# A Strassen level more in the second layer: product 4 by small products, its sums made by ScalarE copies and adding DMAs

## The chip, the cores and the metric

The kernel runs on one core of one Trainium2 chip. The metric is the device time of one execution in microseconds. The engines are named as in the profile: PE is TensorE's matmul, PEld its weight load, DVE is VectorE, ACT is ScalarE, POOL is GpSimd, SP is SyncE, which issues most DMAs.

## The reference

A short causal convolution over time with softmax weights, and then a feed-forward layer with the hardswish function. With B = 8, S = 4096, D = 192, 2048 hidden features:

```python
# _attn_ref
w = softmax(weight)                      # 8 heads x 7 taps
out = np.einsum('hk,bskhg->bshg', w, x_unf)   # causal, 7 taps, 24 channels a head
# _moe_ref, x = out as 32768 x 192
h = x @ w_in                             # 192 x 2048
relu6 = np.clip(h + 3.0, 0.0, 6.0)
g = h * relu6 / 6.0
return (g @ w_out).astype(np.float32)    # 2048 x 192
```

All data are float32. The output is 32768 x 192.

## The kernel before, in words

The tokens are cut into 32 blocks of 1024 (`TB`), each in two halves of 512 (`N`). Block 0 runs on its own path, overlapped with the rounding of the weights. Each of the other 31 blocks has two stretches on TensorE: the first layer (`first_layer`, matmuls of line 432) and the second layer (`second_layer`, line 528).

First layer: the convolved tokens `y` are split into a high and a low part in `y_own` (`split_high` on ScalarE, `split_rest` on VectorE, lines 859 to 863), copied to the other half of the partitions in `y_other` by DMA (`swap_parts`), and multiplied by the parts of `w_in` in 16 units. Units 0 to 7 read `y_own`, units 8 to 15 `y_other`. A unit takes one of four PSUM slots (two banks each); ScalarE takes the relu (line 306), VectorE the gate (line 310), and the result lies in `g`. `g` has four quarters by half of the hidden features and half of the tokens: A11, A21, A12, A22, each 8 chunks of 128 features by 512 tokens. Units 0 to 7 fill A11 and A22, units 8 to 15 A21 and A12.

Second layer: `g @ w_out` by one level of Strassen's method (Winograd's form) over the four quarters of `g` and of `w_out`: seven products of 512 tokens by 96 outputs by 1024 features. The sums of quarters are S1 (in A21's place), S2 (in A11's), S3 and later S4 (in a tile of their own, `S3`). GpSimd makes S3 for the first three pairs of chunks (`g_sums`, lines 468 and 380), VectorE for the last; S1 = A21 + A22 is made by two adding DMAs issued by GpSimd (line 470) and two additions on VectorE (line 472). The sums of weights are made once.

TensorE's array is used as four groups of 32 columns, each with its own 32 rows of PSUM: streams 0 to 3 (`tile_position=(0, j * QS)`). Streams 0, 1 and 2 compute rows 0-31, 32-63 and 64-95 of the products 4, 7, 2, 6 and 3, a matmul of 512 tokens (`plain`) counting as two steps. Products 1 and 5 are cut once more by the same method, in stream 3 (`level_two`): their rows 0-63 as seven small products of 256 tokens and 4 matmuls (`small`, four steps each), rows 64-95 plain. The small products 1 and 2, for one, add onto the same PSUM rows (A), with a copy of A to another place (B) between them. Pieces move between rows of PSUM by ScalarE copies (`copy`, lines 525 and 608 to 611) and VectorE additions (line 400).

The order is written out by hand. `put` gives each matmul the step at which its stream has come to it (`clock`), `do(t, ...)` places a copy, sum or store at step t, less a half. All are sorted by step, stably, and issued in that order; each engine then runs its own in order. The framework adds the semaphore waits from what each instruction reads and writes. Every stream has 82 steps. The second layer uses three of the four PSUM slots, six banks named d, e, b, x_, a and c; B, C and V are rows 96-127 of x_, d and b, A and E rows 96-127 of e and a. In product 1, rows 64-95 are begun by stream 3 in V, copied into e and continued by streams 0, 1 and 2 in turn, each time with a copy of e's rows to the next stream's rows.

Between the matmuls `second_layer` also issues the next block's `split_high`, `split_rest` and `swap_parts` (steps 13, 15 and 18), the small sums of S1 into A22's place for product 5 (`small_sums`, line 637, on VectorE), S2 and S4 (lines 641 and 642, step 38), and what finishes each output.

Of the kernel before, what the change touches and what calls it, by code (L numbers as in the profile page):

```python
# [31 lines left out]
def kernel(  # L32
# [8 lines left out]
    nc = tc.nc  # L41
# [27 lines left out]
    ys = ctx.enter_context(tc.tile_pool(name="ys", bufs=1))  # L69
    ot = ctx.enter_context(tc.tile_pool(name="ot", bufs=1))  # L70
# [50 lines left out]
    y_own = [cst.tile([P, K3, N], F32, name=f"y{n}") for n in range(2)]  # L121
# [4 lines left out]
    w_s = cst.tile([P, 2, 4, NP // 2, QS], F32, name="w_s")  # L126

# [314 lines left out]

    def first_layer(i, jobs):
# [11 lines left out]
        count = 2 * NP  # L455
        for job in jobs.get(-1, ()):
            job()
        for n in range(count):
            unit(n)
            for job in jobs.get(n, ()):  # L460
                job()
# [4 lines left out]
            if n > NP and n % 2:  # L466
                pair = slice(n - NP - 1, n - NP + 1)
                g_sums(nc.gpsimd if n + 1 < count else nc.vector, (3,), range(NP)[pair], 2)
# [24 lines left out]
    def small_weights(to, w):  # L493

        b11, b12, b21, b22 = (
            w_out[:, c::2, w, q * QS : (q + 1) * QS] for c in range(2) for q in range(2)
        )
        t1, t2, t3, t4 = (to[:, n] for n in range(4))
        for o, p, q in ((t1, b12, b11), (t2, b22, t1), (t3, b22, b12), (t4, b21, t2)):
            nc.gpsimd.tensor_tensor(out=o, in0=p, in1=q, op=ALU.subtract)  # L500

    def second_layer(i, between):
        last = i + 1 == NB
        ours = [free_slots.pop(0) for _ in range(3)]
        d, e, b, x_, a, c = (psum[:, 2 * n + k] for n in ours for k in range(2))
# [36 lines left out]
        def small(n, m_, out, start=False):  # L542

            x, w = prod[n]
            sums, ws = (s1[-1], w_s[:, 0]) if n == 1 else (s5, w_s[:, 1])
            x11, x12, x21, x22 = four_parts(x)
            z1, z2, z3, z4 = four_parts(sums)
# [3 lines left out]
            t1, t2, t3, t4 = (ws[:, k] for k in range(4))  # L551
# [4 lines left out]
            for u in range(NP // 2):  # L556
                put(3, 1, lambda u=u: matmul(
                    3, out[:, lo], wm[:, u], xm[:, u], start and u == 0
# [15 lines left out]

        for q in range(NQ):
            plain(q, d, 4, q, every, True)
            before = (1, 6, NP)[q]
            plain(q, c, 7, q, every[:before], True)
            plain(q, e, 1, 2, range(5 + q, 6 + q))
            do(clock[q], copy, out=e[rows(q + 1)] if q < 2 else p1[third], in_=e[rows(q)])  # L580
            plain(q, c, 7, q, every[before:])
            plain(q, a, 2, q, every[:6], True)
# [8 lines left out]
        def level_two(n, p, chunks, order):  # L591
# [25 lines left out]
            for step in order.split():  # L617
                if step[0] == "x":
                    fill(int(step[1]))
                elif step[0] in "lh":  # L620
# [326 lines left out]
```

## Time and profile before

| what | us |
|---|---|
| median of 3 runs (lowest, highest) | 2220.99 (2220.94, 2223.57) |
| the profiled execution, its time | 2220.6 |
| its span, first to last instruction | 2218.5 |
| matmuls of line 528, busy share of the chain | 50% |
| matmuls of line 432, share of the chain | 47% |
| first layer of one block (983.07 on) | 32.87 |
| second layer of one block (1015.94 on) | 35.47 |
| GpSimd's adding DMA, issue to landing | 5.0 |

The page of the profile gives each engine's busy time, the chain of work that ended last followed back to the start, and groups of like instructions with their mean time and the idle time ahead of them. A timeline row reads: start, length, engine, line of the kernel, operation, tile written <- tile read, shape, count, and in brackets the idle time of that engine just before it and what released it. In a table by stretches the columns are: stretch, its length, then busy time and count for PE, PEld, DVE, ACT and POOL, the granted TensorE clock, the busy share of the DMA engines and GB/s. A queue line gives packets, megabytes and the share of 16 DMA engines' time; an issue line the count, the size and the median time to landing.

### The profile page before, as it was taken

What the parts mean: (1) busy time and instruction counts of PE and PEld (TensorE: products, weight loads), DVE (VectorE), ACT (ScalarE), POOL (GpSimd) and SP (SyncE); (2) the same over time, 40 slices, a digit from 0 to 9 for tenths busy, and PEclk for the clock granted to TensorE, in tenths of its full rate; (3) what the DMA queues carried; (4) which work ended last, traced back from release to release, by engine and by line L of the source; (5) the groups of instructions that cost most, each with busy time, mean ns of one, the idle gap of its engine ahead of it and who ended that gap; (6) DMA issues with size and microseconds to landing.
All of it is one profiled execution on the core that took longest, in us unless ns stands there. A gap on an engine that the chain in (4) does not pass through costs nothing.

```text
span 2218.5 us, 49343 instructions
## 1 busy us (share of the span) xinstructions
PE 2211.4 (100%) x21598; PEld 1535.2 (69%) x21598; DVE 1808.9 (82%) x1588; ACT 935.8 (42%) x1172; POOL 827.9 (37%) x706
## 2 busy tenths in 40 slices
PE   9999999999999999999999999999999999999999
PEld 5567776677776677766777667776667776677766
DVE  8878788888888888888888888888888888888866
ACT  7434443344433444433444334443344433344433
POOL 4434442244422344323444224442244432344322
PEclk9999999999999999999999999999999999999999
DMA  7333323433223332243332333322433224333232
GB/s 165 65 71 69 66 37 67 77 63 77 35 58 78 70 70 49 44 77 70 70 62 40 68 74 66 77 35 59 77 68 73 43 49 77 70 70 57 40 59 34
DMA packets 249095, 142.91 MB, mean 64 GB/s; under 512 B 207120, under 2 KB 212240, under 8 KB 248880
## 3 DMA queue, kind: packets, MB, share of 16 engines
q1 hardware_dynamic: 230392, 105.86, 23.7%
q0 software_dynamic: 17248, 33.64, 8.8%
q8 instruction: 169, 2.77, 0.5%
q10 hardware_dynamic: 1240, 0.27, 0.1%
q14 instruction: 46, 0.38, 0.1%
HBM read 31.72 MB, written 25.17 MB: 26 GB/s over the span
## 4 chain that ended last, share of the span: by engine, by line
PE 99%; ACT 0%; DVE 0%; POOL 0%; DMA 0%; issue 0%; POOLq 0%; ACTq 0%; DVEq 0%
PE psum L528 50%; PE psum L432 47%; PE psum L321 2%; PE psum L730 0%; PE psum L738 0%; ACT g L306 0%; DMA y_other<-y 0%; POOL w_in L220 0%; ACT scale L196 0%; ACT sig L193 0%; ACT sig L199 0%; POOL sig L210 0%; ACT w_in L218 0%; DVE y L283 0%; POOLq L942 0%
## 5 line engine op out<-in xcount | busy, mean ns | idle before, releaser
L528 PE MATMUL psum<-g,w_out 128*32 128x512 f32 (+1 forms) x6712 | 967.4, 552 | 0.0
L306 ACT ACTIVATE g<-psum,half 128x1024 f32<-128x1024 f32 x512 | 572.3, 1118 | 494.0 <-PE psum L432 465.8
L310 DVE SCALAR_TENSOR_TENSOR g<-g,psum 128x1024 f32<-128x1024 f32 x512 | 618.8, 1218 | 195.1 <-ACT g L306 194.8
L491 POOL TENSOR_TENSOR s<-g 128x256 f32<-128x256 f32 x248 | 268.8, 1084 | 1252.5 <-DVE g L310 915.9
L528 PEld LDWEIGHTS psum<-g,w_out 128*32 128x32 f32 x6712 | 370.8, 110 | 246.9 <-issue 126.7
L432 PE MATMUL psum<-y,w_in 64*128 64x512 f32 x4608 | 534.8, 388 | 0.3
L432 PE MATMUL psum<-y_other,w_in 64*128 64x512 f32 x4608 | 529.0, 386 | 0.1
L432 PEld LDWEIGHTS psum<-y,w_in 64*128 64x128 f32 x4608 | 428.6, 184 | 121.3 <-issue 26.0
L432 PEld LDWEIGHTS psum<-y_other,w_in 64*128 64x128 f32 x4608 | 431.6, 184 | 91.1 <-DMA y_other<-y 0.5
L528 PE MATMUL psum<-s,w_out 128*32 128x512 f32 (+1 forms) x3272 | 465.4, 570 | 0.0
L806 DVE SCALAR_TENSOR_TENSOR y<-x,c_sb,y 128x1536 f32<-128x1536 f32 x186 | 334.8, 1800 | 2.1 <-ACT y L804 1.0
L380 POOL TENSOR_TENSOR s<-g 128x1024 f32<-128x1024 f32 x93 | 297.8, 3202 | 25.1 <-DVE g L310 25.1
L528 PE MATMUL psum<-g,w_s 128*32 128x256 f32 x1240 | 282.8, 379 | 0.0
L528 PEld LDWEIGHTS psum<-s,w_out 128*32 128x32 f32 x3272 | 153.7, 110 | 80.1 <-issue 48.3
L528 PEld LDWEIGHTS psum<-g,w_s 128*32 128x32 f32 x1240 | 136.4, 110 | 68.3
L380 DVE TENSOR_TENSOR s<-g 128x2048 f32<-128x2048 f32 (+1 forms) x93 | 177.1, 1931 | 1.1
L528 PE MATMUL psum<-s,w_s 128*32 128x256 f32 x744 | 170.7, 379 | 0.0
L491 DVE TENSOR_TENSOR g<-g 128x1024 f32<-128x1024 f32 x124 | 151.7, 1224 | 5.3
L380 DVE TENSOR_TENSOR g<-g 128x2048 f32<-128x2048 f32 x62 | 139.0, 2283 | 0.0
L400 DVE TENSOR_TENSOR p<-psum,p 32x256 f32<-32x256 f32 (+1 forms) x93 | 47.7, 513 | 96.5 <-PE psum L528 95.1
L400 DVE TENSOR_TENSOR results<-psum,results 32x256 f32<-32x256 f32 (+3 forms) x128 | 69.3, 541 | 50.8 <-issue 47.3
L525 ACT COPY psum<-psum 32x512 f32<-32x512 f32 x93 | 51.3, 551 | 135.4 <-PE psum L528 135.4
(88 smaller groups left out, 1089.1 us busy)
## 6 DMA issues: line engine op xcount, KB each, us to landing
y_other<-y SPq DMA_DIRECT2D x124, 384.0 KB, 4.9
g<-g POOLq DMA_DIRECT2D x62, 512.0 KB, 5.0
out_dram<-results SPq DMA_DIRECT2D x378, 64.0 KB, 2.0
x<-in_x_dram SPq DMA_DIRECT2D x53, 388.5 KB, 7.1
g<-in_moe_w_in_dram SPq DMA_DIRECT2D x16, 192.0 KB, 5.7
stage<-in_moe_w_out_dram SPq DMA_DIRECT2D x8, 384.0 KB, 5.7
x<-in_x_dram SPq DMA_DIRECT2D x7, 384.0 KB, 6.5
y_other<-y SPq DMA_DIRECT2D x12, 128.0 KB, 2.3
```

Source lines behind the costliest of these rows:

```text
L306: nc.scalar.activation(r6, h, ACT.Relu, bias=half[:], scale=1.0 / 6.0)
L310: nc.vector.scalar_tensor_tensor(out=g_, in0=g_, scalar=1.0, in1=h, op0=ALU.min, op1=ALU.mult)
L321: lambda p=p: nc.tensor.matmul(out=bank[j * QS : (j + 1) * QS, tokens], lhsT=w_out[:, p, w, cols], rhs=x[:, p, tokens], start=(first and p ...
L380: engine.tensor_tensor(out=o[:, r], in0=a[:, r], in1=b[:, r], op=op)
L400: nc.vector.tensor_tensor(out=out, in0=x, in1=y, op=op)
L432: nc.tensor.matmul(out=psum[:, 2 * slot + k], lhsT=r32(w_in_parts[wn][r, c, s]), rhs=r32(y_other[r, yn, s] if group else y_own[yn][r, s]), ...
L491: engine.tensor_tensor(out=o, in0=p, in1=q, op=op)
L525: streams[3].append((t - 0.5, lambda: fn(*args, **kw)))
L528: nc.tensor.matmul(out=out, lhsT=w, rhs=x, start=start, stop=True, tile_position=(0, j * QS), skip_group_check=True,)
L806: jobs.append(lambda k=k: nc.vector.scalar_tensor_tensor(out=y[:], in0=x[:, :, k : k + N], scalar=c_sb[:, k : k + 1], in1=y[:], op0=ALU.mu ...
```

## The change

Product 4 (A22 times T4, in streams 0 to 2 plain before, 48 steps) is cut once more too. Its rows 0-63 become seven small products of four steps: 1, 2 and 5 in stream 0, 6 and 3 in stream 1, 7 and 4 in stream 2. Its rows 64-95 stay plain and are made in turn by streams 0, 1 and 2 in bank b (`t4`), with two copies between rows. The pieces are put together in a new SBUF tile `p4`, which is added where bank d was. All streams have 81 steps.

The four small sums of A22 are made while the first layer runs its units 8 to 15: ScalarE copies a quarter with its sign into each sum's buffer (`seed`), GpSimd issues DMAs that add another onto it (`onto`). Two of the four come out with the opposite sign; a third set of small weights, `w_s4`, has the signs turned to match. Two of the buffers lie in the memory of `y_own`, taken after unit 7 and given back after the second layer's use of them, so `split_high`, `split_rest` and `swap_parts` move from steps 13, 15 and 18 to 18, 20 and 23. One S3 pair (unit 11) moves from GpSimd to VectorE. Banks x_ and c change places. The small sums of S1 are made later (steps 22.3, 30.7 and 37), stream 3's first fills go ahead of its small products, the copy of V into e moves from step 14 to 9, and the work from step 32 on comes one step earlier.

```diff
+    w_s4 = cst.tile([P, 5, NP // 2, QS], F32, name="w_s4")
...
+    def sums_a22():
+
+        early = [
+            part[:].rearrange("p s n -> p (s n)")[:, : NP * TH // 2]
+            .rearrange("p (u t) -> p u t", t=TH)
+            for part in z_early or y_own
+        ]
+        return early + [z[:, k] for k in range(2)]
...
+        x11, x12, x21, x22 = four_parts(A22)
+
+        def begin_sums():
+            z_early[:] = own_tiles("z")
+            seed(0, x21, 1.0)
+
+        def seed(k, x, sign):
+            nc.scalar.mul(sums_a22()[k], x, sign)
+
+        def onto(k, x):
+            nc.gpsimd.dma_start(out=sums_a22()[k], in_=x, accum_op=ALU.add)
+
+
+        s4_sums = {
+            NP - 1: [lambda: seed(2, x11, -1.0)],
+            NP: [begin_sums, lambda: onto(2, x21), lambda: onto(0, x22)],
+            NP + 1: [lambda: seed(1, x11, -1.0)],
+            NP + 2: [lambda: seed(3, x12, -1.0), lambda: onto(1, sums_a22()[0])],
+            NP + 6: [lambda: onto(3, sums_a22()[1])],
+        }
...
-                g_sums(nc.gpsimd if n + 1 < count else nc.vector, (3,), range(NP)[pair], 2)
+                g_sums(nc.vector if n in (NP + 3, count - 1) else nc.gpsimd, (3,), range(NP)[pair], 2)
...
-        d, e, b, x_, a, c = (psum[:, 2 * n + k] for n in ours for k in range(2))
+        d, e, b, c, a, x_ = (psum[:, 2 * n + k] for n in ours for k in range(2))
...
+        def plain_half(j, bank, n, q, ch, t, start=False):
             x, w = prod[n]
...
+            put(j, 1, lambda: matmul(
+                j, bank[rows(j), halves[t]], w_out[:, ch, w, q * QS : (q + 1) * QS],
+                x[:, ch, halves[t]], start,
+            ))
...
+            if n == 4:
+                z1, z2, z3, z4 = sums_a22()
+                t1, t2, t3, t4, b22 = (w_s4[:, k] for k in range(5))
...
+        A4, E4, B4, C4 = d[first, lo], d[first, hi], d[second, lo], d[third, lo]
+        t4 = b
...
+        def plain_e(q):
+            plain(q, e, 1, 2, range(5 + q, 6 + q))
+            if q == 2:
+                plain_half(q, e, 1, 2, 4, 1)
+            do(clock[q], copy, out=e[rows(q + 1)] if q < 2 else p1[third], in_=e[rows(q)])
+
+        plain(0, t4, 4, 2, (0,), True)
+        plain_half(0, t4, 4, 2, 1, 0)
+        do(clock[0], copy, out=t4[second], in_=t4[first])
+        small4(0, 1, d[first], True)
+        do(clock[0], copy, out=B4, in_=A4)
+        small4(0, 2, d[first])
+        do(clock[0], copy, out=p4[first, lo], in_=A4)
+        plain_e(0)
+        small4(0, 5, d[first, TH:], True)
+        do(clock[0], copy, out=p4[second, lo], in_=E4)
+        plain(0, c, 7, 0, every, True)
+
+        plain(1, c, 7, 1, every[:3], True)
+        for t, chunks in ((0, (2, 3, 4)), (1, (1, 2, 3, 4))):
+            for ch in chunks:
+                plain_half(1, t4, 4, 2, ch, t)
+        do(clock[1], copy, out=t4[third], in_=t4[second])
+        small4(1, 6, d[second])
+        do(clock[1], copy, out=C4, in_=B4)
+        plain_e(1)
+        plain(1, c, 7, 1, every[3:6])
+        small4(1, 3, d[second])
+        do(clock[1] + 1, add, p4[second, lo], B4, p4[second, lo])
+        plain(1, c, 7, 1, every[6:])
+
+        plain(2, c, 7, 2, every, True)
+        plain(2, t4, 4, 2, (5, 6, 7))
+        do(clock[2], copy, out=p4[third], in_=t4[third])
+        small4(2, 7, d[third])
+        do(clock[2], add, p4[second, hi], C4, p4[second, lo])
+        plain_e(2)
+        plain(2, a, 2, 2, every[:2], True)
+        small4(2, 4, d[third])
+        do(clock[2], copy, out=p4[first, hi], in_=C4)
+        plain(2, a, 2, 2, every[2:6])
+
         for q in range(NQ):
-            plain(q, d, 4, q, every, True)
-            before = (1, 6, NP)[q]
-            plain(q, c, 7, q, every[:before], True)
-            plain(q, e, 1, 2, range(5 + q, 6 + q))
-            do(clock[q], copy, out=e[rows(q + 1)] if q < 2 else p1[third], in_=e[rows(q)])
-            plain(q, c, 7, q, every[before:])
-            plain(q, a, 2, q, every[:6], True)
+            if q < 2:
+                plain(q, a, 2, q, every[:6], True)
+            assert clock[q] == 45
...
-        level_two(1, lambda: p1, range(5), "1 x5 6 5 2 7 3 4")
-        do(14, copy, out=e[first], in_=V)
+        level_two(1, lambda: p1, range(4), "x4 half 1 5 6 2 7 3 4")
+        do(9, copy, out=e[first], in_=V)
...
-        for t, n in ((16.2, 1), (16.2, 2), (30.5, 3), (34.5, 4)):
+        for t, n in ((22.3, 1), (30.7, 2), (30.7, 3)):
...
+        do(37, small_sums, s5, S1, (4,), nc.vector)
...
-        do(62, lambda: add(late["p7"], late["u3"], d[m]))
+        do(61, lambda: add(late["p7"], late["u3"], p4[:]))
...
-                between = [(13, split_high), (15, split_rest), (18, swap_parts)]
+                between = [(18, split_high), (20, split_rest), (23, swap_parts)]
```

## The prediction

> **What bounds the kernel now.** I read the page first: busy shares, then the chain that ended last.
>
> ```profile
> span 2218.5 us, 49343 instructions
> PE 2211.4 (100%) x21598; PEld 1535.2 (69%) x21598; DVE 1808.9 (82%) x1588; ACT 935.8 (42%) x1172; POOL 827.9 (37%) x706
> PE 99%; ACT 0%; DVE 0%; POOL 0%; DMA 0%; issue 0%; POOLq 0%; ACTq 0%; DVEq 0%
> ```
>
> TensorE is the chain; every other engine only has to be in time. The chain listed in order gives the stretches of one block; the table by stretches, cut there, shows what each engine does.
>
> ```profile
> 983.14:1015.94 32.80, 32.80 (x292) 26.83 (x296) 26.97 (x23) 17.32 (x16) 23.59 (x21) 1.00 0.18 30
> 1015.94:1051.40 35.46, 35.46 (x386) 21.11 (x386) 29.19 (x26) 11.08 (x19) 2.04 (x1) 1.00 0.47 94
> ```
>
> First layer 32.8 us, second 35.46 us, clock 1.00. The second layer is written as 82 steps in four streams; 35.46 / 82 = 0.43 us a step, so all four streams are full and nothing stops them. One step less is worth 0.43 us only while that stays so: the question is whether the new order still lets TensorE run without a wait. What a wait costs is read from the tightest place, in the timeline of TensorE, its weight loads and ScalarE.
>
> ```profile
> 1028.34 0.59 PE L528 MATMUL psum<-g,w_out 128*32 128x512 f32 x1
> 1028.77 1.46 PE L528 MATMUL psum<-s,w_out 128*32 128x512 f32 x12
> 1029.01 0.55 ACT L525 COPY psum<-psum 32x512 f32<-32x512 f32 x1 [1.27 <-PE psum L528]
> 1029.61 0.11 PEld L528 LDWEIGHTS psum<-g,w_out 128*32 128x32 f32 x1 [0.23 <-ACT psum L525]
> 1029.62 0.13 PEld L528 LDWEIGHTS psum<-s,w_out 128*32 128x32 f32 x3
> 1029.64 0.59 PE L528 MATMUL psum<-g,w_out 128*32 128x512 f32 x1
> ```
>
> Here the matmul that feeds a copy begins its last pass at 1028.34. The copy starts at 1029.01, ends at 1029.56, and the load that waits for it goes at 1029.61. A matmul right behind the first would have been due at 1028.77 and would have got its weights at 1029.61: a copy with no step between costs 0.85 us. This one has two steps (0.86 us) and costs nothing, by 0.01 us. The row at 1029.62 matters as much: loads of another stream, which need no copy, went only after the waiting one. A wait holds what stands behind it in all four streams.
> The Trainium skill ("TensorE: Matmul & The Clock Gate", Step-by-step) says that TensorE's queue pulls weight loads ahead of matmuls in flight while matmuls keep program order. By that a load behind a waiting one might go early; the row at 1029.62 shows that it didn't.
>
> **The change, part by part.** u is one step, 0.43 us; times are from the start of the second layer. The waits named are those that the changed program has as built: the matmuls' waits on ScalarE's count, instruction by instruction.
>
> *Steps.* Product 4 falls from 48 to 44 steps (7 small products of 4, and 16 plain, for 3 x 16), one step from each stream: -0.43 us.
>
> *More, smaller matmuls.* 17 more a block, 34 more passes. Before, 386 loads of 0.11 us (the load rows of line 528) are 42.5 us in a stretch of 35.46: they overlap each other and the matmuls, and where stream 3 runs small products all the way the step is still 0.43 us. Cost 0.
>
> *Wait at step 4.* The early rows of product 4 are copied from rows 0-31 to rows 32-63 of bank b (the same 0.55 us copy). The copy waits for the count raised after the matmuls of step 2, which end at step 4; stream 3's fill of step 4 writes rows 96-127 of the same bank and, as built, waits for that copy. No step between: 0.85 us.
>
> *Wait at step 7.* Small product 1 of P4 ends there in stream 0; its copy (256 wide, 0.34 us, the row at 1023.88 below) must be done before small product 2 adds onto the same rows, next in the same stream. 0.85 - 0.55 + 0.34 = 0.64 us for stream 0. Streams 2 and 3 next issue at step 8, behind it: 0.64 - 0.43 = 0.21.
>
> *Wait at step 9.* The copy from stream 3's bank-b rows into e, moved from step 14 to 9, is followed at step 9 by stream 1's half matmul into bank b, which waits for it: 0.85 us. Stream 3 is now 0.85 + 0.21 + 0.85 = 1.91 us late, with some 0.1 us of small slips 2.0.
>
> ```profile
> 1018.15 1.48 ACT L415 ACTIVATE y<-y 128x1536 fp32r<-128x1536 f32 x1
> 1023.88 0.34 ACT L610 COPY psum<-psum 32x256 f32<-32x256 f32 x1 [1.10 <-PE psum L528]
> 1025.60 0.37 ACT L611 COPY p<-psum 32x256 f32<-32x256 f32 x1 [0.38 <-PE psum L528]
> 1021.92 1.75 DVE L418 TENSOR_TENSOR y<-y,y 128x1536 fp32r<-128x1536 f32 x1
> 1023.59 2.55 DVE L491 TENSOR_TENSOR g<-g 128x1024 f32<-128x1024 f32 x2
> 1029.15 0.43 DVE L400 TENSOR_TENSOR p<-psum,p 32x256 f32<-32x256 f32 x1 [3.00 <-PE psum L528]
> ```
>
> *split_high, moved from 13 to 18.* Its 1.48 us lay in a gap of ScalarE. Now the buffer is taken by two of the sums until step 17, and behind it on ScalarE stands the copy e[third]<-e[second], which stream 3's small product at step 21 waits for. Three copies due at step 17 wait for matmuls that end at step 18, at 18u + 1.6 (the lag of stream 2) + 0.16 = 9.5; then 0.37 + 0.34 + 0.37 + 1.48 + 0.55 gives 12.6, the matmul 12.7. It is due at 21u + 2.0 = 11.0 to 11.1: 1.6 us.
>
> *What is behind that on VectorE.* split_rest (1.75) follows split_high's end at 12.1; then one small sum (1.22) and the new addition from bank d (0.43): 15.5. Small product 3 of P4, in the same bank at steps 25 to 29, waits for that addition. Stream 3's due time is 26u + 2.0 + 1.6 = 14.8: 0.7 us.
>
> *The sums in the first layer.* Five ScalarE copies of 128x1024 (near the 1.12 us of the relu) in units 7 to 10: relu and copy are 2.2 us against a unit's 2.05, a lag under 1 us, and the next user of a PSUM slot comes four units later. ScalarE waited 465.8 us for TensorE in the relu rows, 15 us a block: 0. The S3 pair moved to VectorE is 1.23 us where VectorE idles 0.8 us a unit (1015.09 in its timeline): 0.
>
> ```profile
> 1010.42 1.20 POOL L470 DMA_DIRECT2D g<-g  x1 [0.30 <-POOL s L380]
> 1011.16 2.89 POOL L380 TENSOR_TENSOR s<-g 128x1024 f32<-128x1024 f32 x1
> q1 hardware_dynamic: 230392, 105.86, 23.7%
> q0 software_dynamic: 17248, 33.64, 8.8%
> g<-g POOLq DMA_DIRECT2D x62, 512.0 KB, 5.0
> ```
>
> *Four adding DMAs on GpSimd.* An issue keeps GpSimd 0.74 us (1010.42 to 1011.16). The third waits for the second's landing, and behind it stands S3's third pair (2.9 us), which stream 2 needs at step 8, 3.4 + 1.0 us late: 4.4. The second is issued at about -9.7 (small sums end at -10.5); landing after 5.0 us, or 10 if it queues behind the first, puts it at -4.7 to 0.3, and the pair's end at 2.1 (as before) to 4.8: 0 to 0.4 us. If their 1 KB pieces took as long each as the 2 KB pieces of before, each transfer would move for 5.4 us in place of 2.7, landing at 3.0 and the pair at 7.5: 3.1 us. The two queue lines speak for size: 0.08 ns a byte with mean pieces of 460 B, 0.09 with 1950 B. I take 0.
>
> *Sum.* 0.85 + 0.21 + 0.85 + 0.1 + 1.6 + 0.7 - 0.43 = +3.9 us for 30 blocks; the last has no split: +1.6. 30 x 3.9 + 1.6 = 118.6. The profiled execution took 2220.6 us, its span 2218.5, as good as the median of 2220.99. Forecast 2220.6 + 118 = 2339.
>
> **Rivals.**
> 1. *The copies hold nothing*: the other streams run on while one waits, and 81 steps count: 31 x 0.43 = 13.3, 2207. It decides if a waiting load lets later loads pass for 0.85 us. For it: the streams are full all through the stretch before. Against: the load at 1029.62. Chance 0.05.
> 2. *The first three waits alone*: split_high finds a gap, as when streams 0 and 1 are later than I have them and the copy is in time. 31 x 1.6 = 50, 2270. Against it: 1.48 us in front of a copy with 0.86 us of slack. Chance 0.12.
> 3. *GpSimd late too*: S3's third pair comes 0.4 to 3.1 us late in each block, on top: 2351 to 2435. For it: the third DMA cannot issue before the second lands. Chance 0.18.
> 4. *Weight loads bind*: each of 34 more passes adds its load, 34 x 0.11 x 31 = 116 with the step gained, 2323 without any wait; inside the range. Against it: 42.5 us of loads in 35.46. Chance 0.02.
> The Trainium skill ("TensorE: Matmul & The Clock Gate", Part 3, What overlaps and what doesn't) says that a weight load overlaps matmuls in flight only when the row group differs. By that rival 4 would hold, as all four streams use all 128 rows; the trace disagrees, with those 42.5 us.
>
> **How the numbers follow.** Forecast case 0.63, rivals 0.05, 0.12, 0.18, 0.02. 2339 is the forecast case's; its own range is 2315 to 2360. The range of 2265 to 2405 holds cases 2 and 4 and the lower half of 3; left out are rival 1 and the top of 3, some 0.15. 0.2% (4.4 us) is about what a measurement of this kernel tells from no change: faster 0.05, within it 0.01, slower 0.94.
>
> **What would show it.** Right: second layers of 39.8 us in the chain, first layers still 32.8; TensorE's loads waiting for ScalarE's copies near steps 4, 7, 9 and 21, for VectorE's addition near 26, each by the sizes above; split_high near 10.6 us into the layer; GpSimd's S3 pair done before 4.4. Wrong: second layers of 35.0 us with no wait on a copy (rival 1); 37.1 us (rival 2); loads waiting for GpSimd's sum or a DMA (rival 3); loads end to end with no releaser (rival 4). What would upset it most is a load that passes a waiting one, or adding DMAs of many short pieces.

## The result, and the profile after

| | before | after |
|---|---|---|
| median of the runs, us | 2220.97 | 2437.61 (2435.47 to 2439.95) |
| ratio, 95% interval | | 1.0973 (1.0954 to 1.0992), slower |
| profiled execution, its span, us | 2220.6, 2218.5 | 2436.49, 2434.7 |
| first layer of a block, median, us | 32.87 | 33.33 |
| second layer, median of 31 (the last two; the very last to the start of its last matmul), us | 35.47 (35.47, 35.20) | 41.84 (39.5, 38.44) |

216.6 us slower, where 118 were forecast. The direction is right, the size is not. The page of the changed kernel: engines, GpSimd's DMA queue, the chain.

```profile
span 2434.7 us, 52196 instructions
...
PE 2330.1 (96%) x22652; PEld 1553.6 (64%) x22652; DVE 1959.7 (80%) x1681; ACT 1159.8 (48%) x1545; POOL 846.3 (35%) x803
...
q0 software_dynamic: 58912, 98.65, 24.9%
...
PE 64%; POOL 13%; DMA 12%; ACT 5%; issue 3%; DVE 2%; POOLq 0%; ACTq 0%; DVEq 0%
```

Before, the chain was 99% PE. Now a quarter of it is GpSimd and DMA, against 5% for ScalarE's copies and 2% for VectorE, which are what the forecast was made of. (The chain also runs through them where PE was busy with something else meanwhile: PE's busy share is 96%.) The table by stretches, cut at one block's two layers:

```profile
1002.01:1035.34 33.33, 33.33 (x292) 26.89 (x296) 28.10 (x24) 21.06 (x20) 20.61 (x20) 1.00 0.39 64
1035.34:1077.20 41.86, 38.64 (x420) 21.59 (x420) 32.55 (x27) 14.59 (x27) 5.40 (x4) 1.00 0.53 102
```

Two surprises: the first layer is 0.46 us longer although PE never stops in it, and the second is 6.4 us longer where 3.9 was the sum. The timeline of the weight loads shows the stops of the second layer, which begins at 1035.34 (the bracket is the idle time just before, and what ended it):

```profile
1037.85 0.14 PEld L567 LDWEIGHTS psum<-g,w_out 128*32 128x32 f32 x4 [0.72 <-ACT psum L564]
...
1041.77 0.11 PEld L567 LDWEIGHTS psum<-s,w_out 128*32 128x32 f32 x1 [1.84 <-POOL s L385]
1043.53 0.14 PEld L567 LDWEIGHTS psum<-g,w_out 128*32 128x32 f32 x4 [1.61 <-ACT psum L564]
...
1050.47 0.14 PEld L567 LDWEIGHTS psum<-g,w_out 128*32 128x32 f32 x2 [1.54 <-ACT psum L564]
...
1053.33 0.11 PEld L567 LDWEIGHTS psum<-z,w_s 128*32 128x32 f32 x1 [0.99 <-DVE p L405]
```

Four of the five stand where the prediction named waits: the copies at steps 4 and 9 (the latter with 1.61 us in place of 0.85), the copy behind split_high, VectorE's addition. The second, for S3's third pair from GpSimd, was costed at nothing. GpSimd's own timeline says why it came late:

```profile
1024.60 2.59 POOL L480 DMA_DIRECT2D z<-g  x2
1026.17 3.47 POOL L385 TENSOR_TENSOR s<-g 128x1024 f32<-128x1024 f32 x1
1029.93 1.20 POOL L506 DMA_DIRECT2D g<-g  x1 [0.30 <-POOL s L385]
1037.22 0.90 POOL L480 DMA_DIRECT2D z<-z  x1 [6.08 <-PE psum L567]
1037.80 1.54 POOL L506 DMA_DIRECT2D g<-g  x1
1038.54 3.18 POOL L385 TENSOR_TENSOR s<-g 128x1024 f32<-128x1024 f32 x1
```

The third adding DMA stands 6.08 us, until the second has landed (the name in the bracket is the profile's guess; the third adds what the second brings). The pair behind it begins at 1038.54 and ends at 1041.72, 6.4 us into the layer, not "before 4.4". And SP's queue shows what else was in flight:

```profile
1027.30 0.58 SPq L88 DMA_DIRECT2D x<-in_x_dram  x1
1027.93 1.35 SPq L89 DMA_DIRECT2D x<-in_x_dram  x1
1049.87 0.50 SPq L299 DMA_DIRECT2D y_other<-y  x1
```

The load of the next x, two transfers of 388.5 KB, goes at 1027.30, in the first layer. Before, it stood behind the swap on SP and went at 41.8 us into the block, in the second layer. The change moves the swap from step 18 to 23 and leaves begin_conv at 20: the load now stands ahead of the swap and goes as soon as its buffer is free (VectorE's last reading of the x before ends at 1027.24).

One pair of numbers in the table at the top already points there. The last block but one has no x to load and a split all the same: its second layer took 39.5 us, 2.3 less than the others.

### The profile page after: what moved, and what is told of

It reads as the page before. It is cut to its first block, busy times and chain, and to the rows that moved or that the text cites. A ratio compares the mean times of both kernels' runs of the same rounds, so it can differ in the third digit from the quotient of the medians.

```text
span 2434.7 us, 52196 instructions
## 1 busy us (share of the span) xinstructions
PE 2330.1 (96%) x22652; PEld 1553.6 (64%) x22652; DVE 1959.7 (80%) x1681; ACT 1159.8 (48%) x1545; POOL 846.3 (35%) x803
## 3 DMA queue, kind: packets, MB, share of 16 engines
q0 software_dynamic: 58912, 98.65, 24.9%
## 4 chain that ended last, share of the span: by engine, by line
PE 64%; POOL 13%; DMA 12%; ACT 5%; issue 3%; DVE 2%; POOLq 0%; ACTq 0%; DVEq 0%
PE psum L567 40%; PE psum L437 22%; DMA z<-g 12%; POOL s L527 7%; POOL s L385 3%; POOL z L480 2%; PE psum L326 2%; ACT psum L564 2%; POOL g L506 1%; ACT y L420 1%; DVE g L315 1%; ACT g L311 1%; DVE p L405 1%; ACT p L564 0%; ACT p L705 0%
## 5 line engine op out<-in xcount | busy, mean ns | idle before, releaser
L567 PE MATMUL psum<-g,w_out 128*32 128x512 f32 (+1 forms) x6526 | 1073.2, 519 | 40.6 <-ACT psum L564 40.6
L567 PE MATMUL psum<-s,w_out 128*32 128x256 f32 (+1 forms) x3272 | 717.2, 574 | 40.6 <-POOL s L385 40.6
L567 PEld LDWEIGHTS psum<-g,w_out 128*32 128x32 f32 x6526 | 395.2, 110 | 341.1 <-ACT psum L564 139.9
L437 PE MATMUL psum<-y,w_in 64*128 64x512 f32 x4608 | 548.4, 393 | 0.2
L567 PEld LDWEIGHTS psum<-s,w_out 128*32 128x32 f32 x3272 | 231.6, 110 | 126.8 <-POOL s L385 54.6
L385 DVE TENSOR_TENSOR s<-g 128x1024 f32<-128x1024 f32 (+1 forms) x124 | 267.1, 2175 | 2.1
L385 POOL TENSOR_TENSOR s<-g 128x1024 f32<-128x1024 f32 x62 | 206.4, 3330 | 0.0
L564 ACT COPY psum<-psum 32x512 f32<-32x512 f32 (+1 forms) x217 | 106.3, 490 | 202.9 <-PE psum L567 200.5
L567 PE MATMUL psum<-z,w_s 128*32 128x256 f32 x992 | 178.8, 383 | 16.2 <-DVE p L405 16.0
L423 DVE TENSOR_TENSOR y<-y,y 128x1536 fp32r<-128x1536 f32 (+1 forms) x33 | 55.9, 1694 | 168.5 <-ACT y L420 168.5
## 6 DMA issues: line engine op xcount, KB each, us to landing
x<-in_x_dram SPq DMA_DIRECT2D x53, 388.5 KB, 9.5
```

The lines of the kernel that those rows point to most:

```text
L385: engine.tensor_tensor(out=o[:, r], in0=a[:, r], in1=b[:, r], op=op)
L423: engine.tensor_tensor(out=r32(out), in0=x, in1=high, op=ALU.subtract)
L437: nc.tensor.matmul(out=psum[:, 2 * slot + k], lhsT=r32(w_in_parts[wn][r, c, s]), rhs=r32(y_other[r, yn, s] if group else y_own[yn][r, s]), ...
L564: streams[3].append((t - 0.5, lambda: fn(*args, **kw)))
L567: nc.tensor.matmul(out=out, lhsT=w, rhs=x, start=start, stop=True, tile_position=(0, j * QS), skip_group_check=True,)
```

## The experiments

The runs, in us (E: early x load, in the first layer; half-clock windows as counted in the profiled execution, up to its last matmul):

| what is changed | median | first layer | second layer | half-clock windows |
|---|---|---|---|---|
| before | 2220.7 | 32.87 | 35.47 | 0 |
| before, y_own in the new place | 2235.9 | 33.35 | 35.47 | 0 |
| before, x load ahead of the swap (E) | 2220.8 | 32.87 | 35.47 | 0 |
| after (E) | 2437.6 | 33.33 | 41.84 | 4 |
| after, S3's third pair first (E) | 2459.9 | 33.34 | 42.63 | 7 |
| after, split later (E) | 2428.8 | 33.35 | 41.39 | 15 |
| after, x load behind the swap | 2361.9 | 33.35 | 39.52 | 0 |
| the same, split later | 2338.7 | 33.35 | 38.71 | 0 |
| the same, no early copies | 2313.8 | 33.34 | 37.74 | 0 |
| the same, y_own in the old place | 2347.6 | 32.87 | 39.51 | 0 |
| 81 steps, other order, first try | 2249.7 | 32.87 | 36.45 | 0 |
| 81 steps, other order, second try | 2212.8 | 32.90 | 35.15 | 0 |

**1. The place of y_own alone.**

```diff
-    y_own = [cst.tile([P, K3, N], F32, name=f"y{n}") for n in range(2)]
+    y_own = [yo.tile([P, K3, N], F32, name=f"y{n}") for n in range(2)]
...
+    cst.tile([P, 5, NP // 2, QS], F32, name="room")
```

> The kernel before, with the two y_own tiles taken out of the pool of the constants and put where the changed kernel has them (171968 and 178112 bytes into a partition, where before they lay at 118944 and 125088); y_other and everything behind them move as in the changed kernel. Nothing else is changed, no instruction is added. Theory of the place: the first eight units of a first layer, which read y_own, take 2.10 us in place of 2.04, as in the trace after; 8 x 0.06 = 0.46 to 0.48 us a block, 31 blocks, some 15 us: 2235 us. Rival, that these units are slowed by what ScalarE, GpSimd and the DMAs do more in the changed kernel: 2221 us, units of 2.04 us.

Measured: 2235.92 us (2235.86 to 2236.0), ratio 1.0068 (1.0053 to 1.0083), first layers of 33.35 us, second layers unchanged. The groups of the first layer's matmuls, reading y_own and reading y_other:

```profile
L434 PE MATMUL psum<-y,w_in 64*128 64x512 f32 x4608 | 548.9, 394 | 0.3
...
L434 PE MATMUL psum<-y_other,w_in 64*128 64x512 f32 x4608 | 530.4, 387 | 0.1
```

394 ns a matmul from the new place; in the kernel before it is 388. The tiles behind y_own moved too, y_other among them, but its matmuls take 387 ns against 386. The move alone, with no instruction added, is 15.2 us, and the whole of the first layer's growth. The rival falls.

**2. The x load back behind the swap.**

```diff
-                between += [(20, begin_conv), ...
+                between += [(24, begin_conv), ...
```

> The changed kernel with the load of the next x behind the swap on SP's queue again (begin_conv at 24 in place of 20), as it stood in the kernel before. Theory A: the x load's packets, which in the trace after run 29 to 34 us into the first layer, slow the second adding DMA; without them it lands 1 to 2 us sooner, the third is issued and S3's third pair ends as much sooner, and 0.9 to 1.9 us of each second layer come back: 2437 - 27 to 57 = 2380 to 2410 us. Rival B: the landing is set by the adding DMAs' own 1 KB pieces: within 6 us of 2437.

Measured: 2361.93 us (2361.13 to 2362.79), 75.7 us less than the changed kernel: theory A, and more than it allowed. Its timelines of SP, GpSimd and the weight loads and its table by stretches, in that order (this block's layers begin at 1116.98 and 1150.33):

```profile
1165.03 1.57 SPq L300 DMA_DIRECT2D y_other<-y  x1
1166.64 1.63 SPq L88 DMA_DIRECT2D x<-in_x_dram  x1
```

```profile
1149.07 0.90 POOL L480 DMA_DIRECT2D z<-z  x1 [2.88 <-DMA z<-g]
...
1150.39 3.22 POOL L385 TENSOR_TENSOR s<-g 128x1024 f32<-128x1024 f32 x1
```

```profile
1152.91 0.14 PEld L567 LDWEIGHTS psum<-g,w_out 128*32 128x32 f32 x4 [0.72 <-ACT psum L564]
...
1156.22 0.14 PEld L567 LDWEIGHTS psum<-g,w_out 128*32 128x32 f32 x4 [0.80 <-ACT psum L564]
...
1163.15 0.14 PEld L567 LDWEIGHTS psum<-g,w_out 128*32 128x32 f32 x2 [1.54 <-ACT psum L564]
...
1166.01 0.11 PEld L567 LDWEIGHTS psum<-z,w_s 128*32 128x32 f32 x1 [0.99 <-DVE p L405]
```

```profile
1150.33:1189.85 39.52, 38.05 (x421) 21.72 (x420) 30.71 (x27) 14.59 (x27) 4.17 (x3) 1.00 0.58 112
```

The x load goes behind the swap. The third adding DMA goes 32.1 us into the block instead of 35.2, the pair ends 3.3 us into the layer, and no load waits for GpSimd any more (in one block of the 31 one still does, for 0.5 us). From the end of the second's issue to the third's it is 6.8 us in the median block, 9.9 with the early x load. What is left are waits where the prediction had them, in a second layer of 39.52 us. The DMA queues' lines of the stretch in which the adding DMAs run, first after (1024 to 1038), then here (1139 to 1153):

```profile
q0 software_dynamic: 1255, 1.46, 72.2%
q1 hardware_dynamic: 416, 0.80, 21.6%
```

```profile
q0 software_dynamic: 1435, 2.01, 91.3%
```

The adding DMAs alone fill the 16 engines to 91%. With the x load beside them they get 72%, and P4's first two land after a median of 8.5 us in place of 6.8 (over the whole execution 7.8 in place of 7.2). The Trainium skill ("DMA: Bandwidth & Descriptors", Queues, rings and completion order) says that each DMA engine takes turns between the queues that have work for it, a packet at a time. The two shares fit that, but another way of sharing would give such shares too; the turns themselves no run here tests.

**3. S3's third pair ahead of the third adding DMA.**

```diff
-            NP + 2: [lambda: seed(3, x12, -1.0), lambda: onto(1, sums_a22()[0])],
-            NP + 6: [lambda: onto(3, sums_a22()[1])],
+            NP + 2: [lambda: seed(3, x12, -1.0)],
+            NP + 6: [lambda: onto(1, sums_a22()[0]), lambda: onto(3, sums_a22()[1])],
```

> The changed kernel with the third adding DMA moved behind S3's third pair on GpSimd (both it and the fourth are issued in unit 14's place); what they do is the same. Theory: the hold of 1.7 to 1.9 us at step 8 is GpSimd standing in the third DMA's wait with S3's third pair behind it; now the pair ends some 33 us into the first layer, the wait at 6.4 us of the second layer goes, and 30 x 1.7 to 1.9 = 51 to 57 us come back: 2380 to 2387. Rival 1: the same time is then lost at the next place, because the copies at steps 7 and 9 or the third sum, which small product 6 of P4 reads at step 13, are as late: within 15 us of 2437. Rival 2, that the pair was late for want of its inputs and not of GpSimd: no change at all.

Measured: 2459.91 us (2457.24 to 2464.91), 22 us more. The pair is early and nobody waits for it; but small product 6 of P4 now waits for the third sum itself:

```profile
1282.88 0.11 PEld L567 LDWEIGHTS psum<-z,w_s 128*32 128x32 f32 x1 [2.52 <-DMA z<-z]
...
1291.94 0.11 PEld L567 LDWEIGHTS psum<-z,w_s 128*32 128x32 f32 x1 [1.99 <-DVE p L405]
```

Rival 1, and worse than it. GpSimd's order was not the root: the late landing was, and both things that hang on it are due by step 13, 5.6 us into the layer by the plan.

**4. The split later.**

```diff
-                between = [(18, split_high), (20, split_rest), (23, swap_parts)]
+                between = [(21.2, split_high), (27.2, split_rest), (29, swap_parts)]
```

> The changed kernel with split_high at 21.2 in place of 18 (behind the copies e[third]<-e[second] and C<-B on ScalarE), split_rest at 27.2 in place of 20 (behind the addition that small product 3 of P4 waits for, on VectorE) and the swap at 29 in place of 23. Theory: the two terms that the prediction put at 1.6 and 0.7 us, and that the trace after shows as 1.4 and 0.8, were what stood in front; they go, but a later copy may wait for split_high in their place: -1.3 to -2.2 us a block, 30 blocks, 2371 to 2398 us. Rival: there is no free 1.5 us on ScalarE in this stretch, and wherever split_high stands it holds the copy behind it: within 15 us of 2437.

Measured: 2428.81 us (2420.1 to 2431.91), 9 us less: by the numbers the rival, but the run can't be read that way. The table by stretches, two second layers of it:

```profile
1183.11:1225.80 42.69, 39.84 (x420) 21.57 (x418) 32.85 (x27) 14.59 (x27) 5.39 (x4) 0.96 0.52 100
1259.15:1300.34 41.19, 38.25 (x420) 20.96 (x418) 32.81 (x27) 14.59 (x27) 5.40 (x4) 1.00 0.54 105
```

The layers fall into two kinds, 41.0 and 42.6 us, the longer ones with a granted clock below 1: 15 windows at half clock against 4. (The shorter ones are 0.8 us less than the changed kernel's 41.84.) So the move was tried again without the early x load.

**5. The split later, with the x load behind the swap.** The diff of 4, with begin_conv at 30.

> The changed kernel with the x load behind the swap, and the split moved as in the run before that moved it (split_high at 21.2, split_rest at 27.2, the swap at 29, the x load at 30). In that run the granted clock fell to 0.5 for a window in about every second block, which hid what the order itself did; without the 1.7 us gap at 4.7 us into the layer the clock should stay at 1.0. Theory: the split's wait (1.3 in the trace with the x load behind the swap, at 11.2 to 12.8 us) and VectorE's (0.7, at 15 us) go or shrink to what the later order of ScalarE's copies leaves, which I put at 0.5 us in all: -1.3 us a block, 39 us: 2323. Rival: the wait only changes its place, to the copy or the addition behind the new place of the split: 2350 to 2365.

Measured: 2338.67 us (2337.35 to 2339.4), 23.3 us less than run 2, between theory and rival; second layers of 38.71 us.

```profile
1150.18 0.11 PEld L567 LDWEIGHTS psum<-z,w_s 128*32 128x32 f32 x1 [0.87 <-ACT psum L704]
...
1152.73 0.11 PEld L567 LDWEIGHTS psum<-z,w_s 128*32 128x32 f32 x1 [1.11 <-DVE p L405]
```

The 1.54 us behind split_high are gone, but a wait of 0.87 us and VectorE's of 1.11 stand there now, and neither is the split's. The last block has no split at all, and in run 2 its timelines of ScalarE, the weight loads and VectorE show the same two:

```profile
2328.60 0.34 ACT L704 COPY psum<-psum 32x256 f32<-32x256 f32 x1 [0.67 <-PE psum L567]
2328.99 0.11 PEld L567 LDWEIGHTS psum<-z,w_s 128*32 128x32 f32 x1 [0.87 <-ACT psum L704]
2331.07 0.42 DVE L405 TENSOR_TENSOR p<-psum,p 32x256 f32<-32x256 f32 x1 [2.18 <-PE psum L567]
2331.54 0.11 PEld L567 LDWEIGHTS psum<-z,w_s 128*32 128x32 f32 x1 [1.11 <-DVE p L405]
```

ScalarE and VectorE stand idle there until TensorE's matmuls are done; then the copy C<-B, and later the addition, hold the next load of a small product of P4, as the early copies do: no step between. So of the 2.4 us that run 2 loses between 11 and 16 us into the layer, the split adds only 0.8 (39.52 - 38.71). With the split out of the way a layer still loses 3.24 us (38.71 - 35.47), as much as the last block does without any (38.44 - 35.20).

**6. Without three of the early copies**, with the x load behind the swap. Out: t4[second]<-t4[first], B4<-A4 and e[first]<-V:

```diff
-        do(clock[0], copy, out=t4[second], in_=t4[first])
...
-        do(clock[0], copy, out=B4, in_=A4)
...
-        do(9, copy, out=e[first], in_=V)
...
```

> The changed kernel with the x load behind the swap (2362 us, second layers of 39.52) and without three of its copies: t4[second]<-t4[first] at step 3, B4<-A4 at step 7 and e[first]<-V at step 9. The matmuls that would add onto what they bring start their rows afresh, so those three partial sums are left out of the output. Theory: these three are the waits of the prediction's first terms, 0.85, 0.21 and 0.85 us, and the streams' lag of 1.8 to 2.0 us at 9 us into the layer goes with them: 30 x 1.8 to 2.0 = 54 to 60, 31 blocks 56 to 62: 2300 to 2308 us, second layers of 37.5 to 37.7. Rival 1, that the lag of the first 9 us is the gate of unit 14 or S3's pairs, and the copies only end with it: above 2340. Rival 2, that the split's wait grows by what the streams come earlier, since its place is set by ScalarE's and not by TensorE's work: 2325 to 2345.

Measured: 2313.79 us (2312.44 to 2315.43), 48.1 us less than run 2, where 54 to 62 were expected; second layers of 37.74 us. The streams' lag (time into the layer, less the work issued by then: 0.429 us for a pass of 512 tokens and 0.216 for one of 256, two passes to a matmul, over four streams) is 0.4 us at 9.5 us into the layer, in run 2 1.9. So these copies are 1.6 us of the 1.9, and rival 1 falls. The wait behind the split shrinks no further than to 1.38. Some layers took 38 to 39 us, which is most of the 6 us that are missing; why they did was not followed up.

**7. y_own back in its old place**, with the x load behind the swap.

```diff
-        return [yo.tile([P, K3, N], F32, name=f"{name}{n}", tag=f"y{n}") for n in range(2)]
+        return [cst.tile([P, K3, N], F32, name=f"{name}{n}", tag=f"y{n}") for n in range(2)]
```

> The changed kernel with the x load behind the swap and the two y tiles (and the sums that share their place) at the addresses that they had in the kernel before. Nothing of the order differs from the run with the x load behind the swap. Theory: the place costs 15.2 us wherever it stands: 2362 - 15 = 2347, first layers of 32.87. What is then left is what the prediction worked out, 2339. Rival: part of the first layer's 0.48 us comes from the sums, copies and DMAs that the changed kernel adds: over 2352.

Measured: 2347.61 us (2346.26 to 2347.75), ratio to the kernel before 1.0570 (1.0555 to 1.0586).

```profile
1109.70:1142.59 32.89, 32.89 (x290) 26.91 (x289) 28.07 (x24) 20.98 (x20) 21.71 (x22) 1.00 0.39 59
1142.59:1182.10 39.51, 38.05 (x421) 21.73 (x419) 30.87 (x27) 14.60 (x27) 4.34 (x3) 1.00 0.58 113
```

The place is worth 14.3 us here, 15.2 in run 1. This is the kernel that the prediction had in mind: 126.9 us slower than before, where it had 118.

**8. All 81 steps in an order without zero slack, first try.** What is moved is in the expectation; the core of it:

```diff
-        A4, E4, B4, C4 = d[first, lo], d[first, hi], d[second, lo], d[third, lo]
+        A4, E4, B4, C4 = d[first, lo], x_[first, lo], d[second, lo], d[third, lo]
...
         small4(0, 1, d[first], True)
-        do(clock[0], copy, out=B4, in_=A4)
+        do(7, copy, out=B4, in_=A4)
+        small4(0, 5, x_[first], True)
...
         small4(0, 2, d[first])
...
-        level_two(1, lambda: p1, range(4), "x4 half 1 5 6 2 7 3 4")
-        do(9, copy, out=e[first], in_=V)
+        level_two(1, lambda: p1, range(4), "x4 half 1 5 6 2 7 3 4", c, {2: 8, 5: 4.2})
+        do(12.9, copy, out=e[first], in_=c[rows(3)])
...
-            do(t, small_sums, s5, S1, (n,), nc.vector)
+            do(t, small_sums, s5, S1, (n,), engine)
```

> All 81 steps, with an order in which no copy or addition has to be done before the very next step of the bank that it touches: product 1's partial rows V go to bank c, E4 to the free rows of the bank x_, small product 5 of P4 between its 1 and 2, the e pieces and the copies some two steps apart, product 7's last pieces behind small product 4 of P4; sums 2 and 4 of P4 as subtractions on VectorE in place of ScalarE's seeds with adding DMAs, sums 1 and 3 of product 5 on GpSimd, split_high behind C<-B, x load behind the swap, y at the addresses of the kernel before. Theory: what the changed kernel loses are its waits, not its smaller matmuls or its step count; without them the second layers are 81 x 0.4325 = 35.0 us and 2220.8 - 31 x 0.43 = 2207 us. Rival 1: VectorE, which takes 2.9 us more a block, or GpSimd, comes late in the second half of the layer: 2220 to 2280. Rival 2: the 34 more passes and weight loads a block cost something of their own that the waits hid, up to 0.11 us each: 2207 to 2320.

Sum 4 of P4 enters this one with the wrong sign; its instructions are those of the right one. Measured: 2249.72 us (2249.56 to 2249.82), second layers of 36.45: in the middle of rival 1's range, and inside rival 2's too, between which run 9 decides. VectorE and GpSimd in the middle of the layer:

```profile
1109.68 2.17 DVE L422 TENSOR_TENSOR y<-y,y 128x1536 fp32r<-128x1536 f32 x1 [3.36 <-ACT y L419]
...
1112.79 2.37 DVE L529 TENSOR_TENSOR g<-g 128x1024 f32<-128x1024 f32 x1
```

```profile
1107.84 6.24 POOL L529 TENSOR_TENSOR g<-g 128x1024 f32<-128x1024 f32 x2 [8.92 <-PE psum L569]
```

While GpSimd makes its two sums (1107.84 to 1114.08), VectorE's split takes 2.17 us in place of 1.75, and a sum of 128x1024 2.37 in place of 1.22. Handing GpSimd 2.4 us of VectorE's work cost VectorE 1.6.

**9. The same, second try.** The core:

```diff
-        for t, n, engine in ((24.2, 1, nc.gpsimd), (24.2, 3, nc.gpsimd), (29.2, 2, nc.vector)):
+        for t, n, engine in ((19.3, 1, nc.vector), (19.3, 3, nc.vector), (29.2, 2, nc.vector)):
...
-        plain(2, c, 7, 2, every[:4], True)
+        plain(2, c, 7, 2, every[:1], True)
+        plain_half(2, c, 7, 2, 1, 0)
+        plain(2, c, 7, 2, every[2:4])
...
-        do(43.6, g_sums, nc.vector, (4,), every, 4)
+        do(43.6, g_sums, nc.vector, (4,), every[:4], 4)
```

> The order without zero slack once more, with what its first run showed put right: that one's second layers were 36.45 us, and its waits were 0.3 us at 6.9 us into the layer (copies that waited for stream 2's matmuls of even steps), 0.3 at 15 to 19 us and 0.7 at 19.1 (a copy behind VectorE, whose small sum took 2.37 us in place of 1.22 and whose split 2.17 in place of 1.76 while GpSimd made the two sums that it had been given) and 0.3 at 20.4. Now stream 2 begins with a half matmul so that its steps end with the others', takes chunk 6 of product 4 first, and sums 1 and 3 of product 5 are VectorE's again, in its free stretch at 8 to 11 us; product 3's second half of S3 is made behind the addition that frees bank b; the sign of sum 4 of P4 is put right. Theory: 81 steps without a wait: second layers of 35.0 to 35.2 us, 2207 to 2214 us, faster than the kernel before by 0.3 to 0.6%. Rival: VectorE is full in this layer (33 of 35 us) and holds the steps at another place: second layers of 35.5 or more, 2222 us or more.

Measured: 2212.81 us (2212.3 to 2213.41), ratio 0.9964 (0.9951 to 0.9978): faster than the kernel before, by 7.9 us; the slowest of its five runs is 7 us below the fastest of 25 of the kernel before.

```profile
1047.46:1080.37 32.91, 32.91 (x290) 26.91 (x289) 30.17 (x25) 19.14 (x18) 22.90 (x22) 1.00 0.38 56
1080.37:1115.52 35.15, 35.15 (x422) 21.64 (x420) 30.57 (x29) 14.53 (x27) 1.05 (x1) 1.00 0.48 96
```

35.15 us against 35.47, with 36 more passes a layer than before by the table and PE busy all through. So the step saved is real, and the smaller matmuls and their weight loads cost 0.1 us a layer at most (81 steps of 0.4325 are 35.03); what cost it were waits and landings. This order has two of P4's four adding DMAs, with the x load behind the swap; what the other two would cost in it was not run.

**10. The kernel before with the x load ahead of the swap.**

```diff
-                between += [(20, begin_conv), ...
+                between += [(17, begin_conv), ...
```

> The kernel before with begin_conv at 17 in place of 20, so that the x load stands ahead of the swap on SP's queue and is issued in the first layer, as in the changed kernel; nothing else is changed. Theory: the early x load costs only where an adding DMA has to land soon. Before, only S1's two run then, and what they bring is read some 17 us later: within 3 us of 2221. Rival, that the early load itself costs, for instance by the reads and writes of the same memory by the engines: 2 us or more a block, 2280 us.

Measured: 2220.81 us (2220.61 to 2221.33), ratio 1.0000 (0.9991 to 1.0009). SP's row shows the load 24.9 us into a first layer that begins at 1051.43, where the changed kernel has it at 25.3:

```profile
1076.28 0.58 SPq L87 DMA_DIRECT2D x<-in_x_dram  x1
```

The early load costs nothing by itself. It does slow the adding DMAs here too: S1's two land after a median of 5.8 us in place of 5.0. But nothing is due by then; in the changed kernel the third adding DMA, S3's pair and step 8 stand in line behind the landing.

**11 and 12. y_own a little further on**, in the kernel of run 1, by 32 bytes and, with 56 in place of 8, by 224:

```diff
+    yo.tile([P, 8], F32, name="pad")
     y_own = [yo.tile([P, K3, N], F32, name=f"y{n}") for n in range(2)]
```

> The kernel before with y_own in the changed kernel's place but 32 bytes further (172000 and 178144). Theory: what counts is the address modulo 64: it was 32 before (118944), 0 in the changed kernel's place (171968), and is 32 here: 2221 us, first layers of 32.87. Rival: it is the region, the neighbours or a coarser remainder (160 of 512 before, 448 in the changed place, 480 here): 2236 us, 33.35.

> The kernel before with y_own in the changed kernel's place but 224 bytes further (172192 and 178336), where the remainder by 64 is 32 and that by 512 is 160, both as before. Theory: the remainder by 64 or by 512 decides: 2221 us here; together with the run at 32 bytes it tells which of the two. Rival: it is the region and no remainder: 2236 us in both.

Measured: 2226.74 us (2226.52 to 2227.23) at 32 bytes, 2220.83 (2220.56 to 2221.38) at 224. The matmul groups of the two, in that order:

```profile
L435 PE MATMUL psum<-y,w_in 64*128 64x512 f32 x4608 | 539.5, 390 | 0.2 <-POOL w_in L223 0.2
```

```profile
L435 PE MATMUL psum<-y,w_in 64*128 64x512 f32 x4608 | 534.9, 388 | 0.5 <-POOL w_in L223 0.2
```

It is no matter of the region: 224 bytes further everything is as before. Nor does the remainder by 64 settle it, since both have 32 there and only one is free. A coarser remainder would fit (160 of 512: 388 ns; 480: 390; 448: 394); whether it is one, and which, these places don't tell, and the tiles behind y_own moved by the same bytes.

## Why the prediction was right and wrong, step by step

The sum for copies, split and additions came out; its causes did so only in part. In run 2, where nothing else disturbs, the lag of the streams as defined in 6 can be read step by step against the terms:

| term of the prediction | forecast, us | lag before and after it, run 2 | measured |
|---|---|---|---|
| wait at step 4 | 0.85 | 0 to 0.9 | 0.9 |
| waits at steps 7 and 9, small slips | 0.21 + 0.85 + 0.1 | 0.9 to 2.0 | 1.1 |
| split_high in front of e[third]<-e[second] | 1.6 | 2.0 to 3.5 | 1.5 |
| VectorE's addition behind the split | 0.7 | 3.5 to 4.4 | 0.9 |
| the step gained | -0.43 | | -0.43 |
| sum | 3.9 | | 4.0 (39.51 - 35.47) |

- *A wait holds all four streams*, and *no step between costs 0.85 us*: right, shown by the copies taken out (run 6). Rivals 1 and 2 are out; so is rival 4, since run 9 has the passes and their loads and takes 35.15 us. The "39.8" for the second layers was a slip: 35.46 and 3.9 make 39.4.
- *split_high and what is behind it on VectorE*, 1.6 and 0.7: the sizes hold (1.5 and 0.9), partly by luck. split_high does start 10.7 us into run 2's layer, where 10.6 was named, and it does hold the copy e[third]<-e[second]. But with the split moved away 0.8 us come back and not 2.3 (run 5). Under it lay a copy without a step behind it that the prediction does not name, C<-B. The addition is another such place: the prediction has it late behind split_rest and a small sum, but VectorE stands idle for 2.18 us ahead of the last block's, which costs as much.
- *Four adding DMAs on GpSimd, taken at 0* is the step that failed. Its bounds were 0 and 3.1, and rival 3 had them at a chance of 0.18; it came to 2.3 us a block (41.84 - 39.52), so rival 3 is what happened (without the place some 2423 us, in the part of it that the stated range left out). The third DMA does wait for the second's landing, as it says; what delayed the landing it does not name. With the queues as the prediction had them in mind the term is 0, as forecast: in run 2 the third DMA goes 1.3 us ahead of the layer and the pair ends 3.3 us into it, both inside the ranges given, and a piece of 1 KB takes 113 ns, not as long as one of 2 KB (180). But the prediction moved the swap and never asked what stood behind it on SP. The x load did. It passed the swap, ran beside the second adding DMA, and that set the third, the pair and step 8. With the half-clock windows it is 75.7 us.
- *The first layer, "still 32.8"*: wrong by 0.46 us, 14 to 15 us in all (runs 1 and 7). The prediction looked at what runs in the first layer and not at where the data lie; no row of the trace before could have priced it.
- *The last block, 1.6*: 3.24 (38.44 - 35.20). Without the early copies it is 36.82, so they are 1.6 of it, as forecast; the other 1.6 are the copy C<-B and the addition shown in run 5.
- The seeds (four, 1.05 us each, and not five: ScalarE's row of a first layer goes from 16 to 20), S3's pair on VectorE and the smaller matmuls, all taken at 0: before the wait at step 4 no load of run 2 waits for ScalarE or VectorE, and PE is busy through the first layers. Right.

The account: 126.9 us of waits (run 7 against before), 14.3 of place (run 2 against 7) and 75.7 of the x load (after against run 2) make the 216.9 us between the runs' medians. Against the 118 forecast the miss is 99: 76 of the x load, 14 of the place, 9 of waits.

## What to carry to other kernels

When an instruction is moved to a later place, list what stands behind it on every queue that it leaves, SP's too: what passes it starts earlier, and a transfer that starts earlier takes its share from whatever must land then. A step saved by more and shorter pieces of work is worth having only if each copy between them has some other step of the stream beside it; here the same 81 steps made 2437.6, 2347.6 and 2212.8 us. And an operand that changes its address is a change of its own: time it alone.

## What the runs showed of the hardware that was not expected

- The address of the operand that a matmul streams in changes its time: 388 ns at 118944 bytes into the partition and at 172192, 390 at 172000, 394 at 171968 (matmuls of 64x512), 6 and 15 us in 2221.
- TensorE's granted clock falls to half for 3.41 us at a time, on a fixed grid. In the changed kernel the four windows begin at 136.58, 740.74, 1419.99 and 2174.34 us: 177, 199 and 221 times 3.413 us apart. What PE did in the stretch of the grid just ahead goes with them. Here such a stretch, the window behind it, and a stretch that no window follows (PEclk is the third value from the end):

```profile
737.32:740.74 3.42, 0.97 (x6) 0.15 (x6) 0.99 (x1) 0.00 (x0) 2.39 (x2) 1.00 1.07 195
740.74:744.15 3.41, 2.69 (x24) 1.22 (x26) 0.23 (x1) 0.91 (x2) 0.90 (x1) 0.50 1.03 186
1945.64:1949.05 3.41, 1.55 (x17) 0.49 (x20) 3.32 (x2) 0.55 (x1) 1.99 (x2) 1.00 1.08 190
```

  In the runs with such windows (after, 3 and 4: 26 beginnings, all on their run's grid; two of run 4's windows last twice as long) PE was busy for 28 to 46% of the stretch ahead; of the stretches that no window followed, one had 43.8% and all others 45.7% or more (the first 10 us, before the matmuls run dense, left out). So two stops close together cost half clock only where one stretch of the grid takes in some 1.9 us of them, and of blocks with the same stops only some are struck (4 of 29, 15 in run 4). In the changed kernel their second layers are 1.7 to 2.7 us longer. In runs 2, 5, 6 and 7, their grid taken from the half-clock window after the last matmul, no stretch is under 53%. The Trainium skill ("TensorE: Matmul & The Clock Gate", Part 1, What's actually happening) has a free-running window of 3413 ns and half clock after an idle one; the length agrees. The grid agrees too, but the stretch ahead need not be idle: here a busy share under some 45% was enough, and no single stop of PE in these three runs lasts longer than 2.9 us.
- An adding DMA of 512 KB takes the 16 DMA engines longer in smaller pieces: the changed kernel's took 113 ns for 1 KB, 180 for 2 KB and 341 for 4 KB (medians), which makes 3.6, 2.9 and 2.7 us. In run 2 two in 1 KB pieces, one in 2 KB pieces and parts of two more, 2.01 MB in all, held the engines at 91% for a stretch of 14 us.
- GpSimd at work slows VectorE from 1.22 to 2.37 us for the same 128x1024 sum of two SBUF tiles (run 8; 1.22 again in run 9, where GpSimd makes no sum beside it), though neither waits for the other. It does not slow every instruction: VectorE's gate, which reads one operand from PSUM, takes 1.22 us in the kernel before also where GpSimd computes all the while, and the step of the convolution 1.81 in place of 1.77.
